# Placing side splits by a table of each product's load, spreading the sums, and projecting the first queries inside the down projection

## The chip, the cores and the metric

The kernel runs on one core of one Trainium2 chip. The time is that of one execution on the device in microseconds (us), and a kernel's time is the median of its runs. Beside the times there is one execution taken by the hardware profiler; all rows of the profile come from that one. The engines are TensorE (PE; its weight loads are PEld), VectorE (DVE), ScalarE (ACT), GpSimd (POOL) and SyncE (SP, which issues the transfers). Each engine takes its instructions in the order in which they were queued.

## The reference

The input x has 2048 rows of 1024 numbers, float32. A layer norm gives xn, which feeds two branches.

```python
xn = layernorm(x)
# branch A: linear attention, 32 heads of 32
q, k, v = split(xn @ wqkv)
phi(u) = concat(softmax(u @ w_phi), softmax(-(u @ w_phi)))      # for each head
s = (phi(q) @ (phi(k).T @ v)) / (phi(q) @ sum(phi(k)) + 1e-6) @ wo
# branch B: a gated feed-forward of width 3584
g = silu((silu(xn @ w1) * (xn @ w3)) @ w2)
out = x + s * g
```

## The kernel before

**Numbers and products.** Each float32 operand is split in a high and a low part (`split`, lines 89 to 92: ScalarE copies the high part, VectorE subtracts it from the source), and each product of blocks is three passes of matmuls (high by high, high by low, low by high). The large products are Strassen products in Winograd's form: seven products of blocks in the place of eight, with sums of blocks ahead of them and behind them. One product of gate and up is 12 matmuls of 128x128 by 128x512.

**Stages.** In the profiled execution: a lead-in up to about 75 us (half of x is normed and turned, its Strassen operands are made); **gate and up** to 1166 us (line 514 on); keys and values to 1512 us; **down**, 56 rounds of seven products and a closing round, to about 2062 us; then attention, 16 blocks of 128 rows, to the end. The change touches gate and up, the last rounds of down, and the first block of attention.

**Gate and up.** Two halves of the tokens (tb 0 and 1), in each 28 iterations f over the feed-forward's width, in each iteration seven products, step j = 0 to 6, in this order: A11, A12, S2, S1, S3, S4, A22 (the name is that of the x operand; the weight operands are B11, B21, T2, T1, T3, B22, T4). They sum up in three kinds of PSUM bank: b, a, b, c, b, c, b, of which there are two, one and two (b, a, c). Banks are emptied so: A11, ScalarE copies b to h0 (L551). A12, VectorE adds a to h0 (L553), then ScalarE takes the Silu (L554). S2, ScalarE copies b to u0 (L557). S1, ScalarE copies c to u1 (L564). S3, VectorE adds b to u1 (L566). S4, VectorE adds c to u0 (L568) and multiplies (L569). A22, ScalarE takes the Silu of b (L573), VectorE multiplies (L574), and on odd f adds two results (L578).

Beside that, each iteration prepares the weight operands of the next one (`b_operands`, line 257): GpSimd makes two sums (`b_sums`, L126 and L127), then VectorE and ScalarE do one split behind each product, and GpSimd two subtractions (L266, L268) behind the first and the second of them. The raw weights (`b_load`) have two buffers.

**Side work.** What later stages need is made beside the gate and up products. Pieces of work are put into two dictionaries, `before` and `after`, under a step number, 196 tb + 7 f + j, and run ahead of or behind the product with that number, always ahead of that product's own bank work. `store_quad` (L381) puts one split there, and its store to memory two steps later. Its users:
- `side_x` (L389), the four remaining pairs of x blocks: load, statistics of each block, the reciprocal root (a square root on ScalarE, small operations on VectorE), norm of each, turning on TensorE, two splits, four sums on GpSimd (`a_sums`, L226, all at one step) and five splits at five steps in a row. The pairs start 13 steps apart.
- `side_kv` (L413), eight blocks of the key and value weights, 13 steps apart from step 55: two sums, then seven splits, one each two steps, with two GpSimd subtractions.
- `side_fold` (L430), blocks of the query and key weights, folded with w_phi on TensorE.
- `side_w2` (L451), 14 blocks of w2 in the second half, 11 steps apart: two sums four steps behind the load, then seven splits at 6, 7, 9, 10, 12, 13 and 15 steps.
- `side_split` (L441), 16 blocks of wo, and `side_store` (L476), which has only transfers.

All splits take their output from one pool of 11 buffers (tag q), which their stores give back. From f = 1 on, the order on all five engines is that of the code (`in_order`, L519, up to L587).

**Down and the first block of attention.** A round (L828 on) does the seven products of six matmuls for one pair of token blocks and one block of the width, as in TURN: three from the new round and four from the round before, woven. `product` (L802) empties each bank, mostly by VectorE adding to an accumulator (L825). In the last block of the width (rounds i = 0 to 7), `gate` takes the Silu of the pair that is finished, and the query weights are loaded into what comes free. The closing round (new is None, L835) does the last four products of round 7 and splits the first block of xn for the queries (`split_q`), which was loaded in round 6 (`load_q`, into two buffers of the work pool). The order there is by hand on SP, ScalarE, VectorE and GpSimd; TensorE's is left to the scheduler.

Then come attention's own PSUM pool, `gate` for the last pair, and the first projection of the queries (`project`, 24 matmuls). `queries` (L903) turns a projection into features: VectorE takes maximum and minimum of each head and two differences (L909 to L912), ScalarE the Exp (L915), GpSimd a multiply (L916), VectorE two sums (L920, L924) and small operations, and a last multiply (L930). `attend` (L933) turns the features on TensorE (L940) and multiplies by the key-value state (L946), and `finish` (L953) projects with wo. Block i's `attend` and `finish` run beside the projections of block i + 1, so at i = 0 there are only projections and queries.

Of the kernel before, what the change touches and what calls it, by code (L numbers as in the profile page):

```python
# [28 lines left out]
def tile_kernel(ctx: ExitStack, tc: tile.TileContext, x, wkT, wqT, wv, wphi, wo, w1, w3, w2, out):  # L29
# [64 lines left out]
    def project(ps, xT, w):  # L94

        p = ps.tile([P, 512], F, name="pm", tag="mm")
        n = 0
        for dch in range(ND):
            for a, b in PASSES:
                nc.tensor.matmul(p, xT[dch][:, a], w(dch, b), start=n == 0, stop=n == 3 * ND - 1)  # L100
                n += 1
        return p
# [123 lines left out]
    def a_sums(a, eng):  # L226

        a["S3"] = blk("s3")
        eng.tensor_sub(flat(a["S3"]), flat(a["A11"]), flat(a["A21"]))
        a["S1"], a["S2"], a["S4"] = a["A21"], a["A11"], a["A12"]  # L230
        eng.tensor_add(flat(a["S1"]), flat(a["A21"]), flat(a["A22"]))
        eng.tensor_sub(flat(a["S2"]), flat(a["S1"]), flat(a["A11"]))
        eng.tensor_sub(flat(a["S4"]), flat(a["A12"]), flat(a["S2"]))
# [58 lines left out]
    b_gen = b_operands(rws.pop(0), bo)  # L292

# [86 lines left out]

    def store_quad(step, d, src, name):  # L381

# [4 lines left out]
        at(step, f)  # L387

    def side_x(i, s0):  # L389
# [7 lines left out]
        at(s0, load)  # L397
        for j in range(2):
            at(s0 + 3 + j, lambda j=j: stats(mv[0], j, xt[j]))
        at(s0 + 5, lambda: sd.append(rstd(mv[0])))  # L400
        for j in range(2):
            at(s0 + 6 + j, lambda j=j: norm(mv[0], sd[0], j, xt[j]))
        for m, (n, j, hf) in enumerate((("A11", 0, 0), ("A12", 0, 1), ("A21", 1, 0), ("A22", 1, 1))):
            at(s0 + 8 + m, lambda n=n, j=j, hf=hf: pts.update({n: turn(xt[j][hf])}), before)
            at(s0 + 8 + m, lambda n=n: a.update({n: raw_x(pts[n])}))
            at(s0 + 10 + m, lambda n=n, j=j, hf=hf: store_x(pairs[i][j], hf, a[n]))
        for m, n in enumerate(("A11", "A12")):
            store_quad(s0 + 9 + m, xo_d[1][n][:, i - 4], lambda n=n: a[n], f"xo{n}")
        at(s0 + 15, lambda: a_sums(a, nc.gpsimd))
        for m, n in enumerate(("S3", "S1", "S2", "S4", "A22")):  # L410
            store_quad(s0 + 17 + m, xo_d[1][n][:, i - 4], lambda n=n: a[n], f"xo{n}")

    def side_kv(c, k, s0):  # L413
# [8 lines left out]
        for m, n in enumerate(BNAMES):  # L422
            src = {"B11": 0, "B21": 1, "T2": 4, "T1": 0, "T3": 2, "B22": 3, "T4": 1}[n]
            store_quad(s0 + 6 + 2 * m, wkv_d[c][n][:, :, k], lambda src=src: (r + t2)[src], "wkvo")
            if n == "B11":
                at(s0 + 6, lambda: nc.gpsimd.tensor_sub(r[0], r[3], t2[0]))
            elif n == "B21":
                at(s0 + 8, lambda: nc.gpsimd.tensor_sub(r[1], r[1], t2[0]))
# [22 lines left out]
    def side_w2(kb, kk, s0):  # L451
# [14 lines left out]
        at(s0 + 4, sums)  # L466
        for m, n in enumerate(BNAMES):
            src = {"B11": 0, "B21": 1, "T2": 4, "T1": 0, "T3": 2, "B22": 3, "T4": 1}[n]
            step = s0 + 6 + 3 * m // 2
            store_quad(step, w2_d[kb][n][:, kk], lambda src=src: r[src], "w2o")  # L470
            if n == "B11":
                at(step, lambda: nc.gpsimd.tensor_sub(r[0], r[3], r[4]))
            elif n == "B21":
                at(step, lambda: nc.gpsimd.tensor_sub(r[1], r[1], r[4]))
# [7 lines left out]
    FIRST_STEP = 7  # L482
    for m in range(at_fold, len(folds)):
        side_fold(m, FIRST_STEP + 6 * (m - at_fold))
    for i in range(4, 8):
        side_x(i, FIRST_STEP + 13 * (i - 4))
# [26 lines left out]
    xo = {}  # L513
    for tb in range(2):
        early = {}
        for f in range(NF):
# [11 lines left out]
            bon = {}  # L528
            if not (tb and last):
                b_gen = b_operands(rws.pop(0), bon)  # L530
            hd = h_d[tb][f // 4][:, :, :, f % 2, f % 4 // 2]
            bank = {}
            for j, (b, an, bn) in enumerate(ORDER):
# [11 lines left out]
                if not (tb and last):  # L545
                    next(b_gen)
                for do in after.pop(step + j, ()):
# [36 lines left out]
            bo = bon  # L584
# [186 lines left out]
    wq, wos = {}, {}  # L771
# [15 lines left out]
    def load_q(i):  # L787
        two = []
# [231 lines left out]
```

## Time and profile before

| | us |
|---|---|
| median of three runs | 2480.35 |
| lowest and highest | 2479.05, 2481.3 |
| the profiled execution | 2481.09 |
| its span | 2479.3 |
| PE busy in the lead-in, 0 to 75 | 47.35 |
| PE busy in gate and up, 75 to 1166 | 1070.20 of 1091.00 |
| PE busy in keys and values, 1166 to 1512 | 342.38 of 346.00 |
| PE busy in down, 1512 to 2062 | 545.87 of 550.00 |
| PE busy in attention, 2062 to the end | 405.50 of 417.30 |

The profiled execution is 1.8 us longer than its span, and 0.7 above the median. A row of a stretch (windows) gives its bounds, its length, and then busy time and number of instructions of each engine, the mean granted clock of TensorE, the DMA engines' busy share and GB/s. A row of waits names the waiting engine, its instruction and what ended the wait, then the total, the number and the longest. A row of a timeline has start, duration, engine, line, operation and count, and in brackets the idle time before it and what ended it. A row of a group has line, engine, operation, tiles, shapes and count, then busy us and mean ns.

### The profile page before, as it was taken

The page shows a single profiled execution, that of the slowest core. Times are in us where ns is not written, and L with a number is a line of the kernel's source. Part 1 is how long each engine was busy: PE and PEld are TensorE (multiplying, and loading weights), DVE is VectorE, ACT ScalarE, POOL GpSimd, SP SyncE. Part 2 cuts the span into 40 slices and gives each one's busy share as a digit, 9 for nine tenths or more (in the row PEclk, how much of TensorE's full clock was granted, in tenths as well). Part 3 has the DMA queues.
Part 4 walks back from the last instruction along what each step waited for, and adds up shares of the span by engine and source line. Part 5 has one row for each costly group of instructions (what it writes and reads, how often), then busy time and mean ns, then how long its engine had stood idle before and what let it go on. Part 6 is the DMA issues. An engine that isn't in the chain of part 4 may idle for free.

```text
span 2479.3 us, 35993 instructions
## 1 busy us (share of the span) xinstructions
PE 2411.3 (97%) x13648; PEld 1971.7 (80%) x13648; DVE 1721.3 (69%) x2573; ACT 889.5 (36%) x1551; POOL 673.5 (27%) x481
## 2 busy tenths in 40 slices
PE   5999999999999999999999999999999999999999
PEld 5787788888778787888788788788888887787877
DVE  8577776764577787753566565688878876777776
ACT  6545444443345554442111113422222242222221
POOL 2243544543354554531000000011111112222222
PEclk9999999999999999999999999999999999999999
DMA  8778887755987887754967763623444376222222
GB/s 291 235 267 287 294 258 254 253 191 175 295 287 272 295 285 264 274 195 158 359 225 285 275 210 125 237 99 133 175 174 175 129 258 228 94 73 84 84 84 70
DMA packets 300812, 521.02 MB, mean 210 GB/s; under 512 B 24544, under 2 KB 172000, under 8 KB 298848
## 3 DMA queue, kind: packets, MB, share of 16 engines
q1 hardware_dynamic: 300640, 518.74, 60.6%
q8 instruction: 107, 1.75, 0.3%
q14 instruction: 65, 0.53, 0.1%
HBM read 331.22 MB, written 187.44 MB: 209 GB/s over the span
## 4 chain that ended last, share of the span: by engine, by line
PE 59%; DMA 4%; issue 2%; DVE 1%; ACT 1%; SPq 1%; POOL 0%; ACTq 0%; DVEq 0%; POOLq 0%
PE pm L100 13%; PE bankb L813 11%; PE bankb L622 7%; PE bankb L542 6%; PE bankc L813 6%; PE bankc L622 3%; PE bankc L542 3%; PE banka L813 3%; PE banka L622 2%; PE banka L542 2%; PE po L946 1%; PE pkv L607 1%; DMA xoA<-xo_d0A 1%; PE pt L940 1%; DMA w_d4T<-w2o 1%
## 5 line engine op out<-in xcount | busy, mean ns | idle before, releaser
L92 DVE TENSOR_TENSOR bo<-rw,bo 128x512 fp32r<-128x512 f32 x336 | 298.0, 889 | 126.9 <-ACT bo L91 125.8
L91 ACT CAST bo<-rw 128x512 fp32r<-128x512 f32 x336 | 204.5, 621 | 55.6 <-PE bankb L542 13.1
L813 PE MATMUL bankb<-bo,as 128*128 128x512 f32 x816 | 201.0, 389 | 2.8 <-DVE acc L825 2.8
L823 POOL TENSOR_TENSOR acc<-acc,u 128x512 f32<-128x512 f32 x48 | 62.2, 1296 | 475.3 <-ACT u L822 467.1
L266 POOL TENSOR_TENSOR rw<-rw,t 128x512 f32<-128x512 f32 x56 | 82.6, 1476 | 381.1 <-DVE bo L92 370.7
L100 PE MATMUL pm<-wq,xh 128*128 128x512 f32 x768 | 185.2, 394 | 0.0
L813 PEld LDWEIGHTS bankb<-bo,as 128*128 128x128 f32 x816 | 153.1, 188 | 35.0 <-DVE acc L825 3.3
L542 PE MATMUL bankb<-op0S,bo 128*128 128x512 f32 x672 | 164.9, 394 | 7.7 <-ACT u L557 6.1
L542 PE MATMUL bankb<-op1S,bo 128*128 128x512 f32 x672 | 162.5, 391 | 6.1 <-ACT u L557 5.6
L542 PE MATMUL bankb<-op0A,bo 128*128 128x512 f32 x672 | 160.7, 392 | 6.7 <-ACT bo L91 4.5
L100 PEld LDWEIGHTS pm<-wq,xh 128*128 128x128 f32 x768 | 141.9, 188 | 31.3 <-issue 3.0
L542 PE MATMUL bankb<-op1A,bo 128*128 128x512 f32 x672 | 159.6, 393 | 6.0 <-DVE u L566 3.4
L542 PE MATMUL bankc<-op0S,bo 128*128 128x512 f32 x672 | 162.8, 391 | 0.7 <-ACT u L564 0.4
L542 PE MATMUL bankc<-op1S,bo 128*128 128x512 f32 x672 | 161.5, 389 | 0.5 <-ACT u L564 0.5
L542 PEld LDWEIGHTS bankb<-op1A,bo 128*128 128x128 f32 x672 | 126.7, 189 | 35.3 <-DVE u L566 6.1
L542 PEld LDWEIGHTS bankb<-op0S,bo 128*128 128x128 f32 x672 | 126.1, 189 | 35.7 <-ACT u L557 7.9
L542 PEld LDWEIGHTS bankb<-op1S,bo 128*128 128x128 f32 x672 | 125.5, 188 | 35.0 <-ACT u L557 8.5
L542 PEld LDWEIGHTS bankb<-op0A,bo 128*128 128x128 f32 x672 | 125.5, 188 | 34.0 <-ACT bo L91 4.7
L813 PE MATMUL bankc<-bo,as 128*128 128x512 f32 x576 | 146.5, 389 | 1.3 <-DVE as L92 1.3
L542 PEld LDWEIGHTS bankc<-op0S,bo 128*128 128x128 f32 x672 | 125.7, 188 | 27.7 <-ACT u L564 0.8
L542 PEld LDWEIGHTS bankc<-op1S,bo 128*128 128x128 f32 x672 | 126.1, 188 | 27.0 <-ACT u L564 0.9
L916 POOL TENSOR_TENSOR ez<-e,zb 128x1024 f32<-128x1024 f32 x32 | 77.8, 2431 | 230.2 <-ACT e L915 116.1
(201 smaller groups left out, 4743.4 us busy)
## 6 DMA issues: line engine op xcount, KB each, us to landing
rw<-in_w SPq DMA_DIRECT2D x112, 512.0 KB, 5.2
h_d<-h SPq DMA_DIRECT2D x112, 256.0 KB, 6.5
hr<-h_d SPq DMA_DIRECT2D x56, 512.0 KB, 3.4
xoS<-xo_d0S SPq DMA_DIRECT2D x32, 512.0 KB, 9.8
xoS<-xo_d1S SPq DMA_DIRECT2D x32, 512.0 KB, 3.6
room<-in_w SPq DMA_DIRECT2D x56, 256.0 KB, 5.6
xoA<-xo_d0A SPq DMA_DIRECT2D x24, 512.0 KB, 9.5
xoA<-xo_d1A SPq DMA_DIRECT2D x24, 512.0 KB, 3.8
```

Source lines behind the costliest of these rows:

```text
L91: nc.scalar.copy(hi, src)
L92: (by or nc.vector).tensor_sub(lo, src, hi.bitcast(F))
L100: nc.tensor.matmul(p, xT[dch][:, a], w(dch, b), start=n == 0, stop=n == 3 * ND - 1)
L266: nc.gpsimd.tensor_sub(b11, b22, t2)
L542: nc.tensor.matmul(bank[b], bo[bn][:, w, k], ao[an][:, u, k], start=first and n == 0, stop=LAST[b] == an and n == 11, skip_group_check=True)
L607: nc.tensor.matmul(pkv[sl, m], e[:, m // 4, (m % 4) * P + 32 * h:(m % 4) * P + 32 * h + 32], v[:, 4 * (m % 4) + h], start=first and m == 0 ...
L622: nc.tensor.matmul(bank[b], xo[an][:, u, k], wb[bn][:, w, k], start=an in ("A11", "A12", "S1") and n == 0, stop=LAST[b] == an and n == 11, ...
L813: nc.tensor.matmul(bank[b], t[:, u, pos + k], bos[kb, bn, k][:, w], start=first and n == 0, stop=LAST[b] == an and n == 5, skip_group_chec ...
L823: nc.gpsimd.tensor_add(c, c, u)
L916: nc.gpsimd.tensor_mul(ez, ef, zb[c])
L940: nc.tensor.transpose(pt[:, g, :], e[:, (4 * q + g) * P:(4 * q + g + 1) * P], ident)
L946: nc.tensor.matmul(po[32 * g:32 * g + 32, hh, q * P:(q + 1) * P], kvu[sl, G * c + 4 * q + g], et[sl, g], start=True, stop=True, skip_group ...
```

## The change

It has three parts.

1. **Room.** A planner, `room(step, cost)`, keeps for each step the VectorE cost taken by side work, adds a fixed base for each of the seven products (2.1 on even f or 1.4 on odd f, 0.7, 1.4, 0.7, 0.7, 1.4, 2.1), and gives the first step from `step` on at which the base, what is taken and the new cost come to at most 2.4. A split costs 0.7, the statistics of one block 1.6, the reciprocal root 1.0, a norm 1.0. `store_quad` asks it and returns the step; the chains in `side_x`, `side_kv` and `side_w2` ask for each piece at one step behind the piece before. `side_x` is entered ahead of `side_fold`. The sums of `side_w2` stand three steps behind the load and not four. The starting steps of all blocks are as they were.
2. **Sums.** `a_sums` runs in three parts at three steps. `b_operands` stops once behind the two weight sums, so that those of the next iteration are issued behind the sixth product (S4) of the iteration before, and not behind the first (A11).
3. **First queries.** `load_q` takes one buffer of the q pool in the place of two of the work pool, in round i = 4; the split follows behind round 5, and behind rounds 6 and 7 stand projection and queries of half 1 and of half 0 of block 0, in the PSUM buffers of bank a. The second block is loaded behind round 7. The loop over attention's blocks starts at 1.

```diff
+    def room(step, cost):
+        while True:
+            f, j = divmod(step, 7)
+            base = (2.1 if f % 2 == 0 else 1.4, 0.7, 1.4, 0.7, 0.7, 1.4, 2.1)[j]
+            if base + took.get(step, 0) + cost <= 2.4:
+                took[step] = took.get(step, 0) + cost
+                return step
+            step += 1
     def store_quad(step, d, src, name):
+        step = room(step, 0.7)
...
         at(step, f)
+        return step
...
-            at(s0 + 3 + j, lambda j=j: stats(mv[0], j, xt[j]))
-        at(s0 + 5, lambda: sd.append(rstd(mv[0])))
+            at_ = room(at_ + 1, 1.6)
+            at(at_, lambda j=j: stats(mv[0], j, xt[j]))
+        at_ = room(at_ + 1, 1.0)
+        at(at_, lambda: sd.append(rstd(mv[0])))
...
-        at(s0 + 15, lambda: a_sums(a, nc.gpsimd))
-        for m, n in enumerate(("S3", "S1", "S2", "S4", "A22")):
-            store_quad(s0 + 17 + m, xo_d[1][n][:, i - 4], lambda n=n: a[n], f"xo{n}")
+        at_ = max(at_ + 1, s1 + 7)
+        for m in range(3):
+            at(at_ + m, lambda m=m: a_sums(a, nc.gpsimd, m))
+        at_ += 1
+        for n in ("S3", "S1", "S2", "S4", "A22"):
+            at_ = store_quad(at_ + 1, xo_d[1][n][:, i - 4], lambda n=n: a[n], f"xo{n}")
...
-            store_quad(s0 + 6 + 2 * m, wkv_d[c][n][:, :, k], lambda src=src: (r + t2)[src], "wkvo")
+            at_ = store_quad(at_ + 1, wkv_d[c][n][:, :, k], lambda src=src: (r + t2)[src], "wkvo")
...
-        at(s0 + 4, sums)
+        at(s0 + 3, sums)
+        at_ = s0 + 4
...
-            step = s0 + 6 + 3 * m // 2
-            store_quad(step, w2_d[kb][n][:, kk], lambda src=src: r[src], "w2o")
+            at_ = store_quad(at_ + 1, w2_d[kb][n][:, kk], lambda src=src: r[src], "w2o")
...
         b_sums(b11, b12, b22, t2)
+        yield
...
                     next(b_gen)
+                if j == 5 and rws:
+                    bon = {}
+                    b_next = b_operands(rws.pop(0), bon)
+                    next(b_next)
...
     def load_q(i):
-        two = []
+        two = quad("xf", F)
...
         if new is None:
             in_order(ENG.SP, ENG.Activation, ENG.DVE, ENG.Pool)
             xT = split_q(xf)
-            xf = load_q(1)
...
-            if i == 6:
+            if i == 4:
                 xf = load_q(0)
+            elif i == 5:
+                xT = split_q(xf)
+            elif i > 5:
+                es[7 - i] = queries(project_q(xT, 7 - i, "bka"), 7 - i)
+            if i == 7:
+                xf = load_q(1)
...
-    first = project_q(xT, 0)
...
-    pend = None
-    for i in range(NT):
+    pend = 0, es[0], es[1]
+    for i in range(1, NT):
```

More of the change, by code (lines that the diff above doesn't have):

```diff
@@ L787, in load_q @@
     def load_q(i):
-        two = []
+        two = quad("xf", F)
         for hf in range(2):
-            two.append(work.tile([P, 4, P], F, name="xf", tag="w"))
-            nc.sync.dma_start(two[hf], xn_d[:, 4 * hf:4 * hf + 4, i * P:(i + 1) * P])
-        return two
+            nc.sync.dma_start(two[:, hf], xn_d[:, 4 * hf:4 * hf + 4, i * P:(i + 1) * P])
+        return [two[:, hf] for hf in range(2)]
     def split_q(xf):
```

140 lines of the change are left out of this document (75 added, 65 removed).

## The prediction

> **What bounds the kernel now.** I read the page first, then PE's busy time by stretch, then what PE waited for in the stretches where it isn't full, and last the timelines around the longest waits. The profiled execution took 2481.09 us (its span 2479.3); the median of the three runs is 2480.35, 0.74 lower.
>
> The page's first line, busy time and share of the span:
>
> ```profile
> PE 2411.3 (97%) x13648; PEld 1971.7 (80%) x13648; DVE 1721.3 (69%) x2573; ACT 889.5 (36%) x1551; POOL 673.5 (27%) x481
> ```
>
> The matmul count is not touched by the change, so nothing below 2411 us is in reach; the question is only how many of the 68 us in which PE stands still go. The stretches that the change reaches, with length, then busy time of PE, PEld, DVE, ACT and POOL:
>
> ```profile
> 125.00:240.00 115.00, 109.82 (x523) 90.30 (x522) 85.25 (x135) 58.33 (x104) 46.14 (x32) 1.00 0.79 269
> 240.00:420.00 180.00, 177.35 (x785) 146.32 (x784) 129.31 (x154) 84.92 (x154) 88.40 (x60) 0.99 0.81 269
> 420.00:620.00 200.00, 200.00 (x884) 165.64 (x883) 122.28 (x156) 83.58 (x152) 80.97 (x56) 1.00 0.66 215
> 620.00:740.00 120.00, 113.00 (x485) 91.33 (x484) 82.59 (x97) 50.56 (x92) 51.06 (x34) 0.99 0.86 287
> 740.00:960.00 220.00, 214.51 (x939) 175.32 (x938) 171.15 (x203) 109.79 (x197) 111.63 (x75) 1.00 0.81 283
> 960.00:1160.00 200.00, 199.91 (x881) 165.00 (x880) 129.99 (x165) 88.08 (x159) 79.83 (x56) 1.00 0.61 213
> 2040.00:2120.00 80.00, 74.94 (x451) 59.97 (x450) 56.20 (x99) 24.76 (x35) 17.97 (x8) 0.98 0.58 207
> ```
>
> Gate and up run from 75 to 1165 us. PE is full there from 420 to 620 and from 960 to 1160, so those 400 us hold nothing to win and something to lose. It stands still for 5.2 us in 125 to 240, 2.7 in 240 to 420, 7.0 in 620 to 740, 5.5 in 740 to 960; together 20.3. The transition from down to attention (2040 to 2120) adds 5.1. That is the whole purse: 25.4 us, plus what half-clock stretches cost (below).
>
> PE's waits (waited for: us in total, times, longest): first 125 to 290, then the turn of the half at 640 to 669, then 669 to 960, then 2040 to 2120.
>
> ```profile
> PE bankb L542 <- ACT u L557: 6.1, 4, 2.3
> PE bankb L542 <- DVE u L566: 1.3, 2, 0.8
> PE bankc L542 <- ACT u L564: 0.4, 1, 0.4
> ...
> PE bankb L542 <- ACT u L557: 3.0, 1, 3.0
> PE bankb L542 <- DMA op1A<-xo_d1A: 2.5, 1, 2.5
> ...
> PE bankb L542 <- DVE u L566: 3.4, 5, 1.0
> PE bankb L542 <- ACT u L557: 2.6, 2, 1.5
> PE bankc L542 <- ACT u L564: 0.5, 1, 0.5
> ...
> PE po L946 <- DVE rho L923: 2.5, 1, 2.5
> PE pm L100 <- ACT oT L91: 1.7, 1, 1.7
> ```
>
> The name that keeps coming, u at L557, is ScalarE's copy of S2's bank. S3 takes that bank one product later, so the copy has one product of slack. It is late because of what stands ahead of it on ScalarE: the Silu of L554, which waits for VectorE's add of L553, which stands in VectorE's queue behind the splits. The timeline around the longest of these waits (start, duration, engine):
>
> ```profile
> 658.64 1.77 DVE L92 TENSOR_TENSOR w2o<-room,w2o 128x512 fp32r<-128x512 f32 x1
> 659.94 1.62 POOL L266 TENSOR_TENSOR rw<-rw,t 128x512 f32<-128x512 f32 x1
> 660.33 1.78 DVE L92 TENSOR_TENSOR bo<-rw,bo 128x512 fp32r<-128x512 f32 x1
> 662.03 1.77 DVE L92 TENSOR_TENSOR w2o<-room,w2o 128x512 fp32r<-128x512 f32 x1
> 663.72 0.68 DVE L553 TENSOR_TENSOR h<-banka,h 128x512 f32<-128x512 f32 x1
> 664.43 0.63 ACT L554 ACTIVATE h<-h 128x512 f32<-128x512 f32 x1 [6.08 <-DVE h L553]
> 665.48 0.58 ACT L557 COPY u<-bankb 128x512 f32<-128x512 f32 x1
> 666.11 1.20 PE L542 MATMUL bankb<-op1S,bo 128*128 128x512 f32 x4 [3.01 <-ACT u L557]
> ```
>
> Beside a GpSimd operation a split's subtraction takes 1.77 us, against 0.68 for the add from PSUM at L553. ScalarE stands 6.08 us for that add, and PE 3.01 for the copy behind it.
>
> **The change part by part.** A weight split on VectorE, the model of every side split too, and A22's multiply (busy us, mean ns):
>
> ```profile
> L92 DVE TENSOR_TENSOR bo<-rw,bo 128x512 fp32r<-128x512 f32 x328 | 292.6, 894 | 126.9 <-ACT bo L91 125.8 <-issue 0.8
> L574 DVE TENSOR_TENSOR h<-h,u 128x512 f32<-128x512 f32 x54 | 43.9, 813 | 40.5 <-ACT h L573 40.4
> ```
>
> *Room for the splits.* No operation is added or taken; they move to other products. What decides is VectorE's queue between A22's last multiply and L553's add. A product is 12 matmuls; by the stretch 420 to 620, 884 matmuls fill 200.00 us, so 0.226 each and 2.72 for a product. Count from A22's last matmul: ScalarE's Silu (0.6, as L554's 0.63) and the multiply (0.81) free VectorE at about 1.4; S3 takes the bank at 4 x 2.72 = 10.9. Ahead of that stand, on ScalarE, the Silu 0.63, the copies of two splits at about 0.6 and the copy of L557 at 0.58: 2.4. So the add must end by 8.5 and start by 7.8, which leaves VectorE 6.4 us for splits: 9 at 0.68 (a split alone takes what the L553 row takes), but 3 if each meets GpSimd at 1.77. The order of instructions shows before with up to 10 VectorE operations from one S4 add to the next L553 add, in the iterations with the late waits; after has at most 9 in the w2 part. Between A22's multiply and that add it holds 4 splits in a typical iteration, two of which meet the two GpSimd subtractions of L266 and L268: 2 x 1.77 + 2 x 0.68 = 4.9, inside 6.4. So a copy that is late by VectorE's queue comes in time, and I cost that part of the waits as gone; one that is late otherwise stays.
>
> Two of the waits show the other cause, a split's copy on ScalarE that waits for a transfer out of its ring of buffers, with the copy of L557 behind it; and one of them costs more than its wait:
>
> ```profile
> 940.05 0.62 ACT L91 CAST w2o<-room 128x512 fp32r<-128x512 f32 x1 [3.44 <-DMA wo_d<-wso]
> 272.24 0.62 ACT L91 CAST xoS<-xf 128x512 fp32r<-128x512 f32 x1 [1.03 <-DMA xo_d1S<-xoS]
> 274.69 4.62 PE L542 MATMUL bankb<-op0S,bo 128*128 128x512 f32 x12 [2.15 <-ACT u L557]
> 931.34 2.88 PE L542 MATMUL banka<-op1A,bo 128*128 128x512 f32 x12
> ```
>
> After the stall at 274.69, 12 matmuls took 4.62 us against 2.88: half clock, 1.74 lost. The ring and the number of stores stay as they are, so the 1.5 of the wait at 941 stays. So:
> - x part, 125 to 290: 6.1 + 1.3 + 0.4 + 1.74 = 9.5. The one at 275 (2.15 + 1.74 = 3.9) I halve, since both causes show there and the K/V splits still meet the last x splits in the same iteration. Of the other 5.6 I keep 3.0: the spread chain still issues five S and A22 splits product after product, and the square root's table load still stands on ScalarE. Saved 2.6 + 1.9 = **4.5**, between 0 and 9.5.
> - w2 part, 669 to 960: 3.4 + 2.6 + 0.5 = 6.5. The 1.5 at 941 and another 0.7 stay. Saved **4.3**, between 0 and 6.5.
> - turn of the half, 640 to 669: the 2.5 for the transfer of A12's operand and its neighbour stay, for SP's order of loads there is unchanged. At 666 the same w2 loads arrive late and the same four splits meet GpSimd. Saved **0**, between 0 and 5.5.
> - K/V splits: before every second product, after product after product, six in an iteration. VectorE then has 13 splits at 0.89 and 3.7 for five evictions, 15.3 of 19.0 us: still room, but less. Cost **1.0**, between 0 and the second rival's price.
>
> *Sums of weights and of x.* The two weight sums of GpSimd stand in A22's predecessor (S4) instead of A11. They need only the load, issued an iteration and more earlier, and they cover the same 1.5 us of VectorE each, in S4 and A22 where the planner puts nothing. The x sums are the same four operations over three products. Cost and gain are in the figures above; alone, 0, between -1 and +1.
>
> *First queries in down's last rounds.* Before, projections and queries of block 0 start when down is done, and nothing else is there to do while they run. The transition's chain, half 0 (VectorE, ScalarE), and GpSimd's multiply as a group over this stretch:
>
> ```profile
> 2065.37 1.28 ACT L915 ACT_TABLE_LOAD   x1 [6.20 <-DVE e L912]
> 2066.66 1.06 ACT L915 ACTIVATE e<-e 128x1024 f32<-128x1024 f32 x1
> 2067.75 1.22 DVE L920 TENSOR_REDUCE sums<-e 128x32 f32<-128x1024 f32 x1 [2.45 <-ACT e L915]
> 2070.23 1.22 DVE L924 TENSOR_REDUCE sums<-ez 128x32 f32<-128x1024 f32 x1 [1.25 <-POOL ez L916]
> L916 POOL TENSOR_TENSOR ez<-e,zb 128x1024 f32<-128x1024 f32 x5 | 13.2, 2645 | 45.0 <-ACT e L915 45.0
> ```
>
> After, half 1 is projected behind round 6, half 0 behind round 7, each 24 matmuls (5.4 us) that PE does before in any case. VectorE's chain is four operations on the projection (2.7), a wait for Exp (2.45), a sum (1.22), a wait for the multiply (1.25), then some 3.6 (the second sum at 1.22, the last multiply, as large, and an estimated 1.1 of small operations): 11.2 us a half, in which down's bank evictions stand behind it. A round with 5.4 us of projection behind it gives PE work for that time, so I let round 7 go unhindered, the closing round wait 1 us once, and one of the two first waits of attention stay (po, 2.5) since its input still comes off the queue behind Exp and the multiply. So 3.5 of waits, where before there are the 5.1 of the stretch and some half clock (0.98 granted over 80 us, so at most 1.6; I take 0.9): 6.0. Saved **2.5**, between -7.4 (the two waits, 3.7, twice) and 6.0.
>
> ScalarE loads tables four times more (silu and exp alternate). By the row that is 1.28 each and Exp begins 0.01 us after it. The Trainium skill, "ScalarE: Activation LUTs", section "What ACT_TABLE_LOAD costs", puts a switch at about 2.66 us, for a drain of about 1.38 comes on top, which would be 10.6 us for four where the row says 5.1. The trace does not show the drain; by the page's figure alone, if all of the difference fell on PE, the transition would lose 3.0 instead of saving 2.5.
>
> **Sum.** 2481.1 - 4.5 - 4.3 - 0 + 1.0 - 2.5 = 2470.8 against the profiled execution; 0.74 lower against the median, so 2470.
>
> **The rivals.**
> 1. *The waits only move* (18%). The planner counts 0.7 for a split whatever GpSimd does, and the rows say 1.77 beside it. Then as many stalls come back one product further; only the transition's 2.5 is won: 2478. For it: the mean of 894 ns over all weight splits, well above 0.68. Against: five weight operations of GpSimd in an iteration keep it busy only 40% of the time (80.97 of 200). The Trainium skill, "SBUF — State Buffer", section "SBUF: two separate sides", says that a VectorE operation with two SBUF inputs and a GpSimd operation lock the shared port pair against each other for the whole instruction; the 1.77 agrees, and by that rule room counted in VectorE's time alone is no room.
> 2. *Slower: the K/V splits in a row* (17%). Eight K/V blocks, where before waits of PE are nil (420 to 620). If six splits in a row with their two sums and two subtractions let the copy at L557 come late once a block, as it does at 275 (2.15 us; the longest of the x part was 2.3), that is, with 2.2 each, 8 x 2.2 = 17.6; with the other terms as forecast (without the 1.0) 2469 + 17.6 = 2487. It decides from the point where four of the splits ahead of L553 meet GpSimd (4 x 1.77 = 7.1, over the 6.4), so once the block's own GpSimd operations fall into products A11 and A12. For it: they can, at the first two splits. Against: two at a time is the normal case, 4.9.
> 3. *All waits that the change aims at go* (12%): 9.5 + 6.5 + 6.0 = 22: 2481.1 - 22 - 0.7 = 2458.
> 4. *The transition loses* (5%). VectorE and ScalarE are served in order, so a bank's eviction behind a query stands for Exp, and for the table load in front of it; if the 3.7 of a half fall on PE whole, twice, the 2.5 become a loss of 7.4: 2480. Against: the projections give PE 5.4 us a round to bridge them. The Trainium skill's price of a table switch, above, is a case of this one.
>
> **How the numbers follow.** The forecast has 48%; its own range is 2464 to 2477. About 0.2% is what a measurement of this kernel can tell from no change: 2475.4 to 2485.3. Faster by more: 0.45 of the forecast, 0.12 of rival 3, 0.03 of rival 1: 0.60. Within: 0.03 of the forecast, 0.13 of rival 1, 0.03 of rival 2, 0.04 of rival 4: 0.23. Slower: 0.14 of rival 2, 0.02 of rival 1, 0.01 of rival 4: 0.17. Range 2459 to 2486.
>
> **What the profile after would show.** PE's wait on u L557 in 125 to 290 at about 3 and in 669 to 960 at about 2, no new one in 290 to 620; the wait of 2.5 for the transfer at 647 still there; ScalarE's wait on h L553 under 3 everywhere but at the turn; in 2030 to 2095 one PE wait of 2 to 3 on po and one of about 1 on a bank. Wrong would be: waits on L557 or L566 in 290 to 620 (rival 2), the same total at other times (rival 1), or waits of PE on bank b or c at L813 of over 3 us with VectorE standing for Exp (rival 4).

## The result and the profile after

The changed kernel takes 2488.26 us (median of 9 runs, 2484.75 to 2495.08), the kernel before 2480.99 (9 runs): ratio 1.0030, 95% interval 1.0018 to 1.0042. It is 7.3 us slower; 2470 was forecast, and the range ended at 2486. The profiled execution took 2488.01, its span 2486.2.

The first line of the page after, then the same stretches as before the change (bounds, length, busy time of PE, PEld, DVE, ACT and POOL):

```profile
PE 2410.0 (97%) x13648; PEld 1969.5 (79%) x13648; DVE 1715.1 (69%) x2573; ACT 894.9 (36%) x1555; POOL 672.1 (27%) x481
```

```profile
125.00:240.00 115.00, 113.14 (x538) 93.85 (x536) 85.21 (x129) 59.39 (x103) 47.31 (x33) 1.00 0.80 267
240.00:420.00 180.00, 169.26 (x754) 137.85 (x752) 134.33 (x159) 84.91 (x155) 89.55 (x59) 1.00 0.83 277
420.00:620.00 200.00, 200.00 (x884) 165.62 (x883) 116.52 (x157) 82.25 (x149) 78.24 (x55) 1.00 0.64 206
620.00:740.00 120.00, 111.87 (x482) 90.75 (x481) 77.50 (x95) 50.97 (x93) 50.23 (x34) 0.99 0.87 288
740.00:960.00 220.00, 213.95 (x929) 174.48 (x928) 166.36 (x203) 109.34 (x197) 109.24 (x72) 0.99 0.80 283
960.00:1160.00 200.00, 196.46 (x864) 161.57 (x863) 129.77 (x162) 86.79 (x157) 84.57 (x59) 1.00 0.61 215
2040.00:2120.00 80.00, 77.59 (x471) 62.69 (x470) 58.72 (x101) 33.73 (x45) 18.49 (x10) 1.00 0.64 228
```

PE gains 3.3 us in the first x blocks (113.14 against 109.82) and 2.7 in the transition (77.59 against 74.94). It loses 8.1 between 240 and 420 (169.26 against 177.35) and 3.5 between 960 and 1160. From 420 to 620 nothing changes. So the loss stands in one place of 180 us, and in smaller portions in the w2 part.

PE's waits after, first 265 to 420 us, then the turn of the half at 640 to 676, then 676 to 1166, then the transition (L594 is the copy that was L557, L603 the add that was L566, L601 the copy that was L564, L590 the add that was L553):

```profile
PE bankb L575 <- DVE u L603: 4.5, 3, 2.0
PE bankb L575 <- ACT u L594: 3.8, 2, 3.0
PE bankc L575 <- ACT u L601: 2.4, 2, 1.2
...
PE bankb L575 <- ACT u L594: 3.4, 1, 3.4
PE bankb L575 <- DMA op1A<-xo_d1A: 2.8, 1, 2.8
...
PE bankb L575 <- DVE u L603: 7.6, 5, 2.5
PE bankc L575 <- ACT u L601: 1.4, 2, 1.0
PE bankb L575 <- ACT u L594: 1.4, 2, 0.7
...
PE po L986 <- DMA kvu<-kv_d: 1.9, 1, 1.9
PE bankc L882 <- DVE acc L894: 0.5, 1, 0.5
```

In the w2 part S3's add was the first name before too (3.4 in all, longest 1.0); it is 7.6 now, longest 2.5. The copy of S2's bank has its longest wait, 3.4, at the turn. The longest wait in 265 to 420, by the timeline (VectorE, then GpSimd):

```profile
283.05 1.78 DVE L611 TENSOR_TENSOR h<-h,u 128x512 f32<-128x512 f32 x1
284.87 1.67 DVE L615 TENSOR_TENSOR h<-h,h 128x512 f32<-128x512 f32 x1
286.46 1.28 DVE L92 TENSOR_TENSOR bo<-rw,bo 128x512 fp32r<-128x512 f32 x2
287.66 1.78 DVE L92 TENSOR_TENSOR xoS<-s,xoS 128x512 fp32r<-128x512 f32 x1
289.37 1.77 DVE L92 TENSOR_TENSOR wkvo<-wkv,wkvo 128x512 fp32r<-128x512 f32 x1
291.06 0.68 DVE L590 TENSOR_TENSOR h<-banka,h 128x512 f32<-128x512 f32 x1
...
282.54 1.74 POOL L234 TENSOR_TENSOR xf<-xf 128x512 f32<-128x512 f32 x1
284.36 1.63 POOL L236 TENSOR_TENSOR xf<-xf 128x512 f32<-128x512 f32 x1
287.22 1.68 POOL L270 TENSOR_TENSOR rw<-rw,t 128x512 f32<-128x512 f32 x1 [1.23 <-DVE bo L92]
288.86 1.73 POOL L272 TENSOR_TENSOR rw<-rw,t 128x512 f32<-128x512 f32 x1
290.55 1.71 POOL L126 TENSOR_TENSOR wkv<-wkv 128x512 f32<-128x512 f32 x1
```

An x split (xoS) and a K/V split (wkvo) stand in the same iteration, and so do the x sums (L234, L236), the weight subtractions (L270, L272) and the K/V sums (L126): GpSimd works nearly without a gap, and four of the six VectorE operations ahead of the add take 1.67 to 1.78 us, A22's multiply (L611) and the even add (L615) among them. The add starts at 291.06; the wait of PE behind it is the longest of its row, 3.0, so it was due at about 288.

### The profile page after: what moved, and what is told of

The parts are those of the page before. It is cut to its first block, busy times and chain, and to the rows that moved or that the text cites. A ratio compares the mean times of both kernels' runs of the same rounds, so it can differ in the third digit from the quotient of the medians.

```text
span 2486.2 us, 35893 instructions
## 1 busy us (share of the span) xinstructions
PE 2410.0 (97%) x13648; PEld 1969.5 (79%) x13648; DVE 1715.1 (69%) x2573; ACT 894.9 (36%) x1555; POOL 672.1 (27%) x481
## 4 chain that ended last, share of the span: by engine, by line
PE 82%; DMA 8%; DVE 4%; issue 2%; ACT 2%; SPq 1%; POOL 1%; ACTq 0%; DVEq 0%; POOLq 0%
PE bankb L575 18%; PE pm L100 14%; PE bankb L882 12%; PE bankc L575 8%; PE bankb L659 7%; PE bankc L882 6%; PE banka L575 4%; PE bankc L659 3%; PE banka L882 3%; PE banka L659 2%; DVE bo L92 1%; DMA wkv_d0T<-wkvo 1%; PE po L986 1%; PE pkv L644 1%; PE pt L980 1%
## 5 line engine op out<-in xcount | busy, mean ns | idle before, releaser
L270 POOL TENSOR_TENSOR rw<-rw,t 128x512 f32<-128x512 f32 x56 | 78.7, 1405 | 429.8 <-DVE bo L92 429.7
L100 PE MATMUL pm<-wos,oT 128*128 128x512 f32 x576 | 136.3, 390 | 0.0
```

Of the source, the lines that this page charges most:

```text
L270: nc.gpsimd.tensor_sub(b11, b22, t2)
```

## Experiments: which part

Ratios are to the kernel before, with 95% intervals; 0.001 is 2.5 us.

**The three parts alone.** The first keeps only the queries' part of the diff, the second only the planner with the spread x sums, the third only the weight sums behind S4.

> The kernel before with the third part alone (first queries projected behind rounds 6 and 7). Between matching matmuls, the changed kernel is 10.8 us late at the start of down and 6.9 us late in the third block of attention, so this part should save 3.9 us: 2477 against 2481. All theories on the loss agree here. If it saves nothing, the 3.9 is not the part's own but comes of the state that gate and up leave.

Measured: 0.9986 (0.9975 to 0.9998), 3.5 us less.

> The kernel before with the planner and the spread x sums, but the weight sums issued behind A11 as before, and no early queries. Theory P (packing: side splits product after product fill VectorE's queue, whatever GpSimd does): the whole loss of gate and up, +11, so 2492. Theory G (GpSimd's operations come in unbroken rows and slow each VectorE operation beside them, and the early weight sums close these rows): without the early sums the rows are shorter, so at most +4, 2481 to 2485.

Measured: 1.0058 (1.0039 to 1.0076), 14.4 us more. Theory G is out as it stood: the loss is whole without the early sums.

> The kernel before with the weight sums of the next iteration issued behind S4 alone; side work stays at its steps. Theory E (the early sums by themselves are the loss: they now slow A22's multiply and the odd add to 1.7 us and hold the queue ahead of the next h0 add): +6 to +11, 2487 to 2492. Theory P: within 1 us of 2481. Theory G: between, some +3, since the K/V blocks' own sums still stand apart.

Measured: 0.9977 (0.9967 to 0.9988), 5.7 us less. The queries came out as expected (3.9 less). The planner's loss is nearest to theory P, which had 11. For the early sums no theory had a gain. The three add up to 5.2 more; the change has 7.3.

**Without the planner.** The early sums and the queries together.

> The changed kernel with all side work at the steps of the kernel before (no planner, x sums at one step): early weight sums and early first queries alone. If the two parts add up as measured alone (0.9977 and 0.9986), 0.9963, so about 9 us under the kernel before. If the early sums only gain because they shift a stall that the queries meet again, 0.998 or more.

Measured: 0.9971 (0.9961 to 0.9982), median 2473.49. The two gains add up within the intervals, so the planner costs 1.0030 - 0.9971 = 0.0059, 14.6 us, in the changed kernel.

**The planner for one kind of block** on that base (in the first with the spread sums and the entry of x ahead of the folds, in the last with the w2 sums three steps behind the load):

```diff
-    def store_quad(step, d, src, name):
+    def store_quad(step, d, src, name, plan=False):
+        if plan:
+            step = room(step, 0.7)
```

> Early sums and early queries (the kernel without the planner, 0.9971 of before), plus the planner for the x blocks and the folded query weights alone, with the spread x sums; K/V and w2 work at the steps of before. Theory R, by a count on the order of splits (a ring of 11 buffers, a weight operand free after its product, 7 products on): steps at which a split must wait for a product two or more ahead are 18 in the kernel before, 60 in the changed one, and 19 with this part alone: so within 2 us of 2473.5. Theory X (the waits at 230 to 302 us in the changed kernel are made by the planned x splits): 2479 or more.

Measured: 0.9982 (0.9972 to 0.9991), 2.7 us over the base.

> The same base plus the planner for the K/V blocks alone. Theory R: 27 such steps, 9 more, so 2475 to 2478. Rival 2 of the prediction (one late copy for each of eight blocks): 2485 or more. Theory X: within 2 us of 2473.5.

Measured: 0.9998 (0.9988 to 1.0008), 6.7 over the base.

> The same base plus the planner for the w2 and wo blocks alone, with the w2 sums a step earlier. Theory R: 44 such steps, 26 more, the largest part: 2478 to 2484. Theory X: within 2 us of 2473.5; by the stalls of the changed kernel's own profile (1.8 more in 676 to 965, 3.8 more in 965 to 1195, of which the early sums alone show 3.2), 2474 to 2477.

Measured: 1.0017 (1.0008 to 1.0026), 11.4 over the base. The order (w2, K/V, x) is that of theory R's count, and each part was a little dearer than that theory had it. Together they would be 20.8, against 14.6 for all at once. Where the w2 part pays is seen in PE's waits from 676 to 1166, first with the planner for w2, then on the base:

```profile
PE bankb L562 <- DVE u L590: 8.0, 6, 2.6
```

```profile
PE bankb L546 <- DVE u L574: 5.0, 5, 1.2
```

S3's add again (L590 and L574 here), 8.0 against 5.0, and the longest 2.6 against 1.2; copies on ScalarE add 2.0 with the planner and nothing on the base.

## Experiments: by what

**GpSimd's side sums on VectorE**, in the changed kernel (the same for the K/V and w2 sums and subtractions):

```diff
-            at(at_ + m, lambda m=m: a_sums(a, nc.gpsimd, m))
+            at(at_ + m, lambda m=m: a_sums(a, nc.vector, m))
```

> The changed kernel with the side work's sums and subtractions (x, K/V and w2 blocks, 4 for each block) on VectorE in the place of GpSimd; the weight sums of gate and up stay on GpSimd. Theory G: a GpSimd operation slows about one VectorE operation from 0.68 to 1.77 (1.09), more than the 0.69 that it costs on VectorE itself, so the waits of PE between 230 and 360 us shrink, 2478 to 2483 in all. Theory P: VectorE has 104 operations more of 0.69 in the stretches that are too full already, so 2495 or more.

Measured: 1.0017 (1.0005 to 1.0029), 2487.44: between the two, and not to be told from the changed kernel. Not conclusive, since it brought a wait of its own: VectorE now stood in the turn of the half for the w2 load, and PE behind it (the longest wait is the last number):

```profile
PE bankb L576 <- DVE u L604: 20.8, 11, 11.4
```

**K/V splits two steps apart**, in the changed kernel:

```diff
-            at_ = store_quad(at_ + 1, wkv_d[c][n][:, :, k], ...
+            at_ = store_quad(at_ + (2 if n != BNAMES[0] else 1), wkv_d[c][n][:, :, k], ...
```

> The changed kernel with the K/V splits planned at two steps behind the one before, as their spacing was, and not at one; the planner stays. Rival 2 of the prediction (K/V splits in a row are the loss) and theory R: the waits of TensorE between 265 and 420 us (12.8 us with half clock) fall to about the 5 of the kernel before, so 2480. If the loss is in the x or w2 part, or in VectorE's packing elsewhere, 2486 or more.

Measured: 1.0051 (1.0037 to 1.0064): no gain, rather a loss. Spreading the K/V splits, with the blocks at their place, does not bring the time back, against the second rival of the prediction.

**The ring of split buffers.** All splits share 11 buffers, so I tried the ring from four sides: one buffer less in the kernel before; weight splits behind their product's bank work in the changed one; stores one step earlier on the base without the planner; and the same at the split's own step.

```diff
-    qp = pool("q", 11)
+    qp = pool("q", 10)
```

> The kernel before with 10 split buffers in the place of 11, nothing else. Theory R: 3 side splits in 7 products are then the limit, where K/V and w2 parts have 3.5 and more, so waits of TensorE on u L557 and u L566 come up in the stretches that had none (290 to 620, 960 to 1160): 10 us or more longer. Theory P: the ring is no limit, VectorE has the same work in the same products, within 3 us of the kernel before.

Measured: 1.0148 (1.0134 to 1.0161), 36.7 us more.

```diff
-                if not (tb and last):
-                    next(b_gen)
+                if tb == 0 and f == 0:
+                    next(b_gen)
...
                         hs += [(even_d, 1, even), (hd, 1, h1)]
+                if (tb or f) and not (tb and last):
+                    next(b_gen)
```

> The changed kernel with each weight split (7 in an iteration) issued behind the bank work of its product and not ahead of it, from the second iteration on. Theory R (the ring of 11 split buffers: a split that finds the ring full waits on ScalarE until TensorE has read the oldest operand, and the bank work queued behind it comes late; with 7 weight splits in 7 products only 4 side splits fit before a split waits for a product that is not yet done): a weight operand then holds its buffer one product less, so room for one or two more, and the waits of TensorE between 265 and 420 us and at 990 to 1020 shrink by half or more: 2479 to 2483. Theory P (VectorE has too many splits in a product, whatever the ring): the number of operations in a product is the same, 2486 to 2490.

Measured: 1.0023 (1.0015 to 1.0032), 1.7 under the changed kernel, inside both intervals. That is theory P's number, but the same edit costs 9.9 us of its own on another base (the last run of this group), so it does not decide between P and R.

```diff
-            at(step + 2, lambda: nc.sync.dma_start(d, t.bitcast(F)))
+            at(step + 1, lambda: nc.sync.dma_start(d, t.bitcast(F)))
```

> Early sums and early queries, no planner, and each side split's store issued one step behind the split and not two, so that its buffer comes back 2.7 us sooner. If the ring's waits for stores (some 35 us of ScalarE's waits) reach TensorE, 2 to 4 us less, 2470. Theory R as counted has nearly all late steps wait for weight operands and not for stores: within 1.5 us of 2473.5. SyncE takes its queue in order, so an early store may hold loads behind it: then slower.

Measured: **0.9912** (0.9899 to 0.9924), median 2459.80: 14.6 us less than its base, more than any theory said.

> Early sums, early queries, no planner, and each side split's store issued at the split's own step. Theory R: another 2.7 us sooner, so some gain, 2455 to 2460. Against it SyncE takes its queue in order and would stand for each split, with loads behind it; then 2462 or more.

Measured: 0.9914 (0.9900 to 0.9928). One step earlier is all that there is to win.

> The kernel before with the store one step earlier and nothing else. Theory R: the ring is the limit in the kernel before too, so most of the 13.7 us that this brought on top of the other two parts: 2467 to 2472. If the early weight sums had to be there for it (their subtractions free operands sooner): 2476 or more.

Measured: 0.9950 (0.9937 to 0.9963), 12.4 less than the kernel before, by this line alone.

> Early sums, early queries, no planner, store one step earlier, and the weight splits behind their product's bank work (a weight operand holds its buffer one product less). Theory R: ScalarE's split copies wait 21.5 us for TensorE with the earlier store alone; this takes most of that away, but few waits of TensorE are left between 75 and 1165 us (15 us with half clock, 5 of them not the ring's), so 2452 to 2459. If the ring is no longer a limit: 2459 to 2462.

Measured: 0.9952 (0.9937 to 0.9967), 9.9 more than with the earlier store alone. Moving the weight splits is a loss here; why, no run tells.

The ring is seen in ScalarE's copies of weight splits from 75 to 1166 us (busy, mean ns, idle time ahead of them and what ended most of it): before, then with 10 buffers, then without the planner with the earlier store.

```profile
L91 ACT CAST bo<-rw 128x512 fp32r<-128x512 f32 x328 | 199.8, 621 | 55.6 <-PE bankb L542 13.1 <-DMA xo_d1S<-xoS 5.1 <-DMA wkv_d1T<-wkvo 3.8
```

```profile
L91 ACT CAST bo<-rw 128x512 fp32r<-128x512 f32 x322 | 196.8, 621 | 109.8 <-PE bankc L542 22.8 <-PE bankb L542 21.9 <-PE banka L542 14.4
```

```profile
L91 ACT CAST bo<-rw 128x512 fp32r<-128x512 f32 x328 | 199.5, 621 | 42.3 <-PE bankb L546 6.4 <-DMA w_d5T<-w2o 4.6 <-DMA w_d0T<-w2o 4.6
```

A split's copy has no operand from PE's banks. What it waits for there is that PE has read the operand in the buffer that comes next (a weight operand has no store; its buffer comes back when PE is done with it). A row prints only its three largest releasers, so 13.1, 59.1 (22.8 + 21.9 + 14.4) and 6.4 can't be compared; added up over all copies of splits that wait for one of PE's banks, it is 47.3 us, 136.1 and 21.4. What such a wait does to a bank's eviction shows in the changed kernel's timeline at 301 us:

```profile
301.25 0.62 ACT L91 CAST wkvo<-wkv 128x512 fp32r<-128x512 f32 x1 [2.07 <-PE bankc L575]
...
301.89 0.69 DVE L92 TENSOR_TENSOR wkvo<-wkv,wkvo 128x512 fp32r<-128x512 f32 x1 [1.92 <-ACT wkvo L91]
...
302.50 0.68 DVE L603 TENSOR_TENSOR u<-bankb,u 128x512 f32<-128x512 f32 x1
...
303.24 0.97 PE L575 MATMUL bankb<-op0A,bo 128*128 128x512 f32 x3 [2.04 <-DVE u L603]
```

The K/V split waits until S4 is done, S3's add stands behind it on VectorE though its bank had been ready since S4 began, and A22 waits 2.04 for the add.

**Is the ring the planner's cost?** The changed kernel whole, with the earlier store:

> The changed kernel whole, with each side split's store issued one step behind the split. Theory R (the planner loses because its splits in a row find the ring of 11 buffers full): with buffers back 2.7 us sooner the planner's loss against the kernel without it (14.8 us with stores at two steps: 2488.3 against 2473.5) falls to 5 or less, so 2465 or less, beside 2459.8 without the planner. Theory P (VectorE is too full in the planned products, whatever the ring): the loss stays, 2459.8 + 12 to 15, so 2472 to 2475.

Measured: 0.9977 (0.9968 to 0.9985), 2476.33. The changed kernel gains 13.2 by the line, but the planner's cost stays: 0.9977 - 0.9912 = 0.0065, 16 us. So theory R falls as this expectation states it: stores one step sooner do not take away the planner's loss, and the ring is a limit that both orders pay. Buffers that PE has still to read are not ruled out, for the copies of splits wait 32.4 us for PE's banks in this run and 21.4 without the planner. What is left besides are places of the planned order, and two were undone, one upon the other:

```diff
-        at(s0 + 3, sums)
+        at(s0 + 4, sums)
```

> The changed kernel with the earlier store and the w2 sums four steps behind their load, as before, not three. Theory Q (GpSimd takes its queue in order; at the turn of the half the first w2 sums stand ahead of the weight sums, wait 21 us for their load, and the row of seven GpSimd operations that follows slows the five VectorE operations ahead of the add at L553): the turn's waits fall from 11.3 to some 3 to 8, so 2468 to 2473. If the loads are late anyway, within 1.5 us of 2476.3.

Measured: 0.9981 (0.9972 to 0.9990): no gain in time. The row of events of theory Q is there, as the next section shows, but undoing it is worth nothing that can be measured here.

```diff
-        side_kv(m // 4, m % 4, FIRST_STEP + 48 + 13 * m)
+        side_kv(m // 4, m % 4, FIRST_STEP + 58 + 13 * m)
```

> The same, and each K/V block starts 10 steps later, behind the last planned x splits. Theory M (the planner delays the fourth x block into the first K/V block, and there both blocks' GpSimd operations and splits stand in one iteration; 7.8 us of waits between 265 and 420): 5 to 7 us less than the run beside it. Theory P (the planner's density by itself): within 2 us of the run beside it.

Measured: 0.9948 (0.9936 to 0.9961), 8.2 less than the run beside it; theory M had 5 to 7. The stretch from 265 to 420 us in the changed kernel with the earlier store, then with K/V ten steps later, then without the planner:

```profile
265.00:420.00 155.00, 149.67 (x650) 122.58 (x649) 116.29 (x137) 72.93 (x134) 80.72 (x53) 0.99 0.82 279
```

```profile
265.00:420.00 155.00, 153.21 (x676) 126.57 (x675) 105.20 (x134) 71.97 (x130) 76.86 (x52) 1.00 0.83 278
```

```profile
265.00:420.00 155.00, 154.21 (x680) 127.07 (x679) 104.62 (x137) 73.51 (x133) 70.64 (x49) 1.00 0.81 273
```

With nearly the same number of operations (137, 134 and 137), VectorE is busy 116.29, 105.20 and 104.62 us: the 11 us are operations made slow by GpSimd beside them. The fourth x block and the first K/V block still meet with K/V ten steps later: between two copies of A11's bank (278 to 305 us and 277 to 298) ScalarE copies nine side splits in both runs, in the same order, five of x and four of K/V. What goes is GpSimd's row beside them. GpSimd with K/V at its place, then ten steps later:

```profile
268.18 1.29 POOL L457 TENSOR_TENSOR wkv<-wkv,t 128x512 f32<-128x512 f32 x1 [6.93 <-DVE wkvo L92]
269.43 1.74 POOL L230 TENSOR_TENSOR s<-xf 128x512 f32<-128x512 f32 x1
```

```profile
260.78 1.29 POOL L230 TENSOR_TENSOR s<-xf 128x512 f32<-128x512 f32 x1
...
281.49 1.30 POOL L457 TENSOR_TENSOR wkv<-wkv,t 128x512 f32<-128x512 f32 x1 [0.69 <-DVE wkvo L92]
```

With K/V at its place, the x sums (L230 to L236) stand in GpSimd's queue behind the K/V block's first subtraction (L457), which waits for that block's first split. From 268 us on GpSimd then works without a gap up to 281, and the row meets A22's multiply and the splits: VectorE needs 18.0 us, from 268.4 to 286.4, for the 14 operations ahead of the add of A12's bank. At 0.68 each they would be 9.5, so an estimated 8.5 are GpSimd's; two K/V splits among them, which move away as well ten steps later, would be 1.4. Ten steps later the x sums run from 261 to 270 us, ahead of all that. PE's wait of 3.1 us for the copy of S2's bank is gone, one of 1.8 for S3's add stays, and PE does 676 matmuls in the stretch in the place of 650; 26 at 0.226 us are 5.9 of the 8.2. So this place costs by GpSimd's row far more than by the number of splits (theory P). It is about 6 of the planner's 16 us; where the rest of the 8.2 stands, the traces do not tell.

That is with the earlier store. With stores two steps behind the split, the ring comes on top: the planner for x alone and for K/V alone lose as many matmuls from 265 to 420 us (635 and 636, against 666 on their base), with VectorE busy 106.38 and 104.12 us, against 104.63. ScalarE's copies of splits wait 22.4 and 15.2 us there for stores, against 8.4. With x alone such a wait stands right ahead of the copy of S2's bank (L593 there), and PE waits 6.93 us for it:

```profile
272.98 0.62 ACT L91 CAST wkvo<-t 128x512 fp32r<-128x512 f32 x1 [1.88 <-DMA xo_d1A<-xoA]
273.50 0.58 ACT L593 COPY u<-bankb 128x512 f32<-128x512 f32 x1
...
274.13 4.76 PE L574 MATMUL bankb<-op0S,bo 128*128 128x512 f32 x12 [6.93 <-ACT u L593]
```

What is left of the planner's cost (0.9948 against 0.9912, 8.9 us) is not settled. Counted in matmuls it lies in w2: from 676 to 1166 us PE does 2115 with K/V later and 2156 without the planner, 41 or 9.3 us. S3's add comes late there (4.0 us of PE's waits against 1.1); whether by density, by GpSimd or by the loads, no run took apart.

## Why the prediction was wrong

**Room for the splits: the step that failed.** It counted 7.8 us saved (4.5 + 4.3 - 1.0), and the planner alone cost 14.4. The working checked one queue, the splits ahead of L553's add, for one typical iteration with two of four splits beside GpSimd, and let "a copy that is late by VectorE's queue" come in time on that. Three things were left out.
- The planner doesn't only spread, it delays. The chain of a block asks for each piece behind the piece before, while blocks begin at fixed steps, so the last x block slid further into the first K/V block: its sums stand at steps 67 to 69 in the place of 61, and so behind that block's first subtraction in GpSimd's queue, its last five splits at 71 to 75 in the place of 63 to 67. There four of six operations ahead of L590 met GpSimd, among them A22's own multiply, which I had at 0.81 and which took 1.78. I had the number for it (4 splits at 1.77 are over 6.4) and put it under the second rival, eight times over, in the wrong place.
- The second gate was not checked. S3's add (L566, after it L603) has the same slack of a product, and the base table gives S1 and S3, the products ahead of it, the most room (0.7). There the waits grew: from 3.4 to 7.6 after 676 us.
- All splits share 11 buffers. I used the ring only for two waits, which I let stay. In the run with the planner for x alone a wait for the ring stands ahead of PE's longest wait.

**The saving in the first x blocks** was right in its mechanism: PE gains 3.3 between 125 and 240, and 3.1 with the planner alone (112.95 busy). That the saving ends where the blocks meet is the point above.

**The weight sums** were costed at 0, between -1 and 1; alone they are worth 5.7. The gain is spread out: by 1166 us PE is 34 matmuls ahead (4789 against 4755), 11 of them before 265 us and 10 at the turn of the half from 640 to 676. At the turn GpSimd shows a reason: before, then with the early sums alone, then in the changed kernel with the earlier store.

```profile
653.82 1.29 POOL L126 TENSOR_TENSOR room<-room 128x512 f32<-128x512 f32 x1 [19.44 <-DMA room<-in_w]
...
656.43 1.73 POOL L126 TENSOR_TENSOR rw<-rw 128x512 f32<-128x512 f32 x1
```

```profile
645.55 1.28 POOL L126 TENSOR_TENSOR rw<-rw 128x512 f32<-128x512 f32 x1 [15.88 <-DMA rw<-in_w]
...
649.15 1.28 POOL L126 TENSOR_TENSOR room<-room 128x512 f32<-128x512 f32 x1 [0.94 <-DMA room<-in_w]
```

```profile
653.16 1.29 POOL L126 TENSOR_TENSOR room<-room 128x512 f32<-128x512 f32 x1 [21.47 <-DMA room<-in_w]
...
655.79 1.75 POOL L126 TENSOR_TENSOR rw<-rw 128x512 f32<-128x512 f32 x1
```

Before, the weight sums of the next iteration (rw) stand in GpSimd's queue behind the first w2 sums (room), which wait for a late load. Issued a product earlier they pass it, and the row of GpSimd operations is over sooner. The planner puts the w2 sums one step earlier too, and takes that back. Prediction step 2 asked only which products the sums slow, and not what they stand behind. That this place is the main part of the 5.7 is not shown: 10 matmuls are 2.3 us, the turn varies by more than that with the same code (below), and undoing it in the last pair of runs did not move the time. Why the early sums gain stays open.

**The turn of the half** was costed at 0 and is 1.3 us worse by PE's waits from 640 to 676 (3.4, 2.8 and 0.8, against 3.0, 2.5 and 0.2). The early sums alone leave PE busy for 32.04 us there and the planner alone for 28.03, against 30.17 before, so two effects may cancel. But the run with the first queries alone, whose code up to there is that of before, has 27.12, so differences of 3 us in this stretch can't be read.

**First queries**: 2.5 forecast, 3.5 measured, 2.7 in PE's busy time; right, though not by its own list of what stays. The wait on po for VectorE's chain went, and one of 1.9 for the load of the key-value state came in its place. ScalarE's table loads cost PE nothing that shows, as the row of before said:

```profile
2062.60 1.28 ACT L850 ACT_TABLE_LOAD   x1
2063.89 1.06 ACT L850 ACTIVATE e<-e 128x1024 f32<-128x1024 f32 x1
2064.97 1.28 ACT L821 ACT_TABLE_LOAD   x1
2069.42 1.06 ACT L821 ACTIVATE acc<-acc 128x1024 f32<-128x1024 f32 x1 [3.17 <-DVE acc L894]
```

Exp starts 0.01 after its load, and the load back stands in time in which the silu waits for VectorE anyway. The Trainium skill ("ScalarE: Activation LUTs", section "What ACT_TABLE_LOAD costs") adds a drain of about 1.38 us for a switch; this trace has no room for one between load and activation, and the part alone is a gain of 3.5, where by that figure a loss of 3.0 was estimated.

**The rivals.** The first (waits only move) had the right part of the mechanism, GpSimd beside VectorE, and no price for the case that rows get denser. (The 40% against it is right, but it is made of four weight operations in an iteration and those of the K/V blocks, not of five weight operations.) The Trainium skill's rule there ("SBUF — State Buffer", section "SBUF: two separate sides") agrees with the rows at 283 to 291 us: 1.67 to 1.78 beside GpSimd, 1.28 for the two weight splits together that start in its gap. The second had the sign, the K/V blocks, and even the size, with the wrong count: one meeting of x and K/V and a dearer w2 part, not eight late copies. The sign that the prediction names for it came, waits on S2's copy and S3's add between 290 and 620, but none of them after 420.

## The version that beats both

Early weight sums, early queries, no planner, and stores one step behind their split: 0.9912 of the kernel before (0.9899 to 0.9924), 2459.80 us against 2481.41 beside it. PE waits 1.1 us for S3's add in 676 to 1166, and the waits of the x part are nearly gone. The gain of the change's two good parts is 7 us; the store line brings twice that.

## What to carry to other kernels

A planner that knows one engine's time moves load onto what it does not know: here GpSimd's operations, whose company makes a VectorE operation of 128x512 with both inputs in SBUF 1.1 us longer (up to 1.78 against 0.68), and a shared ring of buffers. When work is spread by delaying it, look first at which blocks it then meets and what it stands behind in each engine's queue, and check every gate of the iteration, not the one that was late. And before placing work anew, look at how long its buffer is held: issuing a store one step sooner was worth more than all the rest.

## What the runs showed of the hardware

One split buffer of 11 (128 partitions of 4 KB) is worth 36.7 us, and 2.7 us of earlier stores 12 to 15. SyncE loses nothing by standing for each split with its store (0.9914 against 0.9912). VectorE's time for 137 operations of one size (128x512) was 116.29 us in one order and 104.62 in another; the timelines show up to 1.78 us for such an operation beside GpSimd and 0.68 without.
